# Moving the maximum and the low part's subtraction of the first MLP's weight conversions from VectorE to GpSimd

## The chip, the cores and the metric

One core of one Trainium2 chip runs the whole program. The metric is device time in microseconds of that core, the median over several runs. The engines are named as in the profile: PE (matmuls), PEld (its weight loads), DVE (VectorE), ACT (ScalarE), POOL (GpSimd) and SP (SyncE, which issues most of the DMAs).

## What is computed

An attention with 32 global and 512 local tokens for each of 4 batches and 8 heads of 64, with a window of 32 for the local queries, and then two MLPs over the 2176 rows of the result. Cut to what matters:

```python
s_g = scale * q_g @ k_all.T;  out_g = softmax(s_g) @ v_all
s_l = [scale * q_l @ k_g.T, where(|i-j| <= 32, scale * q_l @ k_l.T, -1e9)]
out_l = softmax(s_l) @ [v_g, v_l]
x = concat([out_g, out_l]) as rows of 8*64 = 512
h = x @ w_in          # 512 -> 2048, first MLP
x = max(0.01*h, h) @ w_out
h = x @ w2_in         # second MLP
x = (h - tanh(h)) @ w2_out
```

The weights of both MLPs come as 64-bit floats: each element is a low and a high 32-bit word.

## The kernel before

**Split numbers.** Every large matmul is made of three: an operand is held as a high part (rounded to the type that PE reads at full rate) and a low part (what the rounding left), and high times high, low times high and high times low are summed in PSUM. `split_w` makes the two parts of a weight: a copy on ACT (L138) and a subtraction (L139).

**Conversion.** A weight block of 128 rows by 512 arrives as pairs of words. `convert_w` turns it into 32-bit floats in five steps, each over 128x512: the absolute value of the high word on ACT (L123, into `wf`), the maximum with a tiny number (L124), a shift and mask (L125, into `wt`), the sign from the high word (L129) and the top bits of the low word (L132, back into `wf`); the last four are on DVE. `wf` has two buffers and `wt` one. `in_job` converts and splits a block of the first MLP's input weights into a `win` tile that stays; `out_job` does the same for the output weights, into `woh` (four buffers) and `wol` (three), which are also stored to DRAM by two SP DMAs (L711, L712) for later use. There are 16 blocks of each kind, so 32 such conversions. The second MLP's 32 blocks go through the same `convert_w`, called from `w2_job`, and are split later by `w2_place`.

**Attention.** It goes in 32 steps (`stage(s)`, counted from 0): a step is a pair of heads in one half of a sequence. For each, PE transposes keys and queries (`kps`, `qps`) and makes the scores (`sps`); DVE takes their minimum (L386; from step 10 on L392 does this with the mask); ACT makes the exponentials in four pieces (L399); DVE adds a small number to the sums and takes the reciprocals (L408, L409); the normalization of `e` is on POOL for steps 0 to 7 (two instructions of L413) and on DVE from step 8 (four of L418); PE transposes the result (`ptps`, L429), which is copied to `pt` by DVE or ACT (L432, L434); PE multiplies with the values (`avps`), and ACT and DVE split the outcome into `xh` and `xl` (L459, L461). Global queries run beside it (`sgps`, `gtps`, `gavps`; L528 to L532 on DVE, L529 on ACT, L567 and L568 for their split). `e` has two buffers that the steps take in turn.

**Order of the work.** The first ten steps run alone, with one `in_job` in each from step 2 on. Then the first MLP starts, with the rest of the attention woven between its matmuls: an item is one block of 128 hidden rows for a chunk of up to 512 tokens (`h`, then g on ACT and DVE by L201 to L203, and two items later `y`). During the first chunk each item also brings one `in_job`, for a block eight items ahead, and one `out_job`, for the block whose `y` comes about an item later. The second MLP's conversions follow in later items. PE's order is fixed by the order of the code up to the second MLP; on DVE, ACT, POOL and SP a scheduler places the instructions by its own costs, and each engine then runs its own list strictly in order. `converted` places a conversion after the last `avps` split and the last exponential issued so far.

Of the kernel before, what the change touches and what calls it, by code (L numbers as in the profile page):

```python
# [14 lines left out]
TINY = 2.0**-15  # L15
# [6 lines left out]
def kernel(  # L22
# [14 lines left out]
    nc = tc.nc  # L37
# [31 lines left out]
    def win_tile(f):  # L69
        t = persist.tile([128, 2, DM], F32R, tag=f"win{f}", name=f"win{f}")  # L70
        win_h[f], win_l[f] = [t[:, k].rearrange("p (k n) -> p k n", k=ND) for k in range(2)]
        return t
# [21 lines left out]
    def f32(t):  # L94
        return t.bitcast(F32)
# [18 lines left out]

    nw = [0]

    def convert_w(raw):
        hw, lw = raw[:, :, 1], raw[:, :, 0]
        t = mlp.tile([128, DM], I32, tag="wt", name="wt", bufs=1)
        w = mlp.tile([128, DM], F32, tag="wf", name="wf", bufs=2)  # L120
        nw[0] += 1

        nc.scalar.activation(w, hw.bitcast(F32), AF.Abs)  # L123
        nc.vector.tensor_scalar_max(w, w, TINY)  # L124
        nc.vector.tensor_scalar(  # L125
            out=t, in0=w.bitcast(I32), scalar1=3, scalar2=0x3FFFFFFF,
            op0=ALU.logical_shift_left, op1=ALU.bitwise_and,
        )
        nc.vector.scalar_tensor_tensor(  # L129
            out=t, in0=hw, scalar=-0x40000000, in1=t, op0=ALU.bitwise_and, op1=ALU.bitwise_or  # L130
        )
        nc.vector.scalar_tensor_tensor(  # L132
            out=w.bitcast(I32), in0=lw, scalar=29, in1=t, op0=ALU.logical_shift_right, op1=ALU.bitwise_or
        )
        return w

    def split_w(w, hi, lo, lo_engine):
        nc.scalar.activation(hi, w, AF.Copy)  # L138
        lo_engine.tensor_sub(lo, w, f32(hi))  # L139
# [6 lines left out]
    def wo_split(f, w):  # L146
        hi = mlp.tile([128, DM], F32R, tag="woh", name="woh", bufs=4)
        lo = mlp.tile([128, DM], F32R, tag="wol", name="wol", bufs=3)
        split_w(w, hi, lo, nc.vector)
        wo_t[f] = hi, lo  # L150

    def wo_fetch(f):
# [538 lines left out]
    def converted(raw):  # L691


        with tc.issue_after(last_av[0].ins), tc.issue_after(last_exp[0].ins):
            return convert_w(raw)

    def in_job():
        if in_raw:
            f, raw = in_raw.pop(0)
            w = converted(raw)  # L700
            t = win_tile(f)
            split_w(w, t[:, 0], t[:, 1], nc.vector)

    def out_job():
        if out_raw:
            f, raw = out_raw.pop(0)
            wo_split(f, converted(raw))
            hi, lo = wo_t[f]

            def store():  # L710
                nc.sync.dma_start(out=wo_dram[f][:, 0], in_=f32(hi))  # L711
                nc.sync.dma_start(out=wo_dram[f][:, 1], in_=f32(lo))  # L712

            later.append(store)
            out_load()
# [7 lines left out]
    def w2_job():  # L723
        if w2_raw:
            kind, f, raw = w2_raw.pop(0)
            with tc.issue_after(anchor[0].ins):
                w = convert_w(raw)
            dst = (w2i_dram if kind == "in" else w2o_dram)[f]
            later.append(lambda: nc.sync.dma_start(out=dst, in_=w))
        if w2_jobs:  # L730
            kind, f = w2_jobs.pop()
            w2_raw.append((kind, f, load_w(kind, w2_in if kind == "in" else w2_out, f)))
# [93 lines left out]
    if True:  # L826
# [16 lines left out]
        for pp in range(PRE):  # L843
            for op in stage(pp):
                op()
            in_load()
            if pp == 0:
                load_kq(2)
            if pp == 1:
                load_v(1)  # L850
            if pp >= 2:
                in_job()
            if pp == PRE - 2:
                out_load()
                out_load()
# [28 lines left out]
        for n in range(len(items) + 8):  # L884
            ph, c, f = items[n] if n < len(items) else (3, 0, 0)
            one = items[n - 1] if 0 < n <= len(items) else (3, 0, 0)
            if ph == 1:
                if c == 0:
                    in_load()
                    in_job()  # L890
                    if f > 0:
                        out_job()
                elif c == 4 and f == 0:
                    while gtodo:
                        gtodo.pop(0)()
                    att_ctx.close()
                    p2 = ctx.enter_context(tc.tile_pool(name="p2", bufs=1))
                    for k in range(NF - 1):
                        wo2_t.append([p2.tile([128, ND, 128], F32R, name=f"wo2{x}{k}") for x in "hl"])
                    wo2_t.append([x[1][:, :, 512:] for x in (xh, xl)])  # L900
                    x2_load(0, 0)
                    x2_load(0, 1)
                if c == 4 and 2 <= f < 2 + ND:
                    x2_split(0, f - 2)
            elif ph == 2 and order2.index(c) + 1 < 5:
                nx = order2[order2.index(c) + 1]
                if f in (2, 3):
                    x2_load(nx, f - 2)
                if 5 <= f < 5 + ND:
                    x2_split(nx, f - 5)  # L910
# [73 lines left out]
```

## Time and profile before

| | us |
|---|---|
| median of 3 runs | 955.41 |
| lowest and highest of the runs | 955.14, 955.56 |
| profiled execution: span from first to last instruction | 953.1 |
| PE busy in the span | 924.0 |
| DVE busy | 649.1 |
| ACT busy | 536.9 |
| POOL busy | 36.4 |

For the profiled execution the profile gives its span alone; the runs' median is 2.3 us above it. A busy time is an average over stretches with different limits, so the stretches are looked at one by one: the table of windows gives the busy time of each engine in each of them, the list of waits tells what ended an engine's idle time, and the timeline shows single instructions in order. The rows of these views that are used stand in a section of their own below.

### The profile page before, as it was taken

The page shows a single profiled execution, that of the slowest core. Times are in us where ns is not written, and L with a number is a line of the kernel's source. Part 1 is how long each engine was busy: PE and PEld are TensorE (multiplying, and loading weights), DVE is VectorE, ACT ScalarE, POOL GpSimd, SP SyncE. Part 2 cuts the span into 40 slices and gives each one's busy share as a digit, 9 for nine tenths or more (in the row PEclk, how much of TensorE's full clock was granted, in tenths as well). Part 3 has the DMA queues.
Part 4 walks back from the last instruction along what each step waited for, and adds up shares of the span by engine and source line. Part 5 has one row for each costly group of instructions (what it writes and reads, how often), then busy time and mean ns, then how long its engine had stood idle before and what let it go on. Part 6 is the DMA issues. An engine that isn't in the chain of part 4 may idle for free.

```text
span 953.1 us, 15441 instructions
## 1 busy us (share of the span) xinstructions
PE 924.0 (97%) x5436; PEld 769.9 (81%) x5436; DVE 649.1 (68%) x1429; ACT 536.9 (56%) x1223; POOL 36.4 (4%) x67
## 2 busy tenths in 40 slices
PE   7788999999999999999999999999999999999998
PEld 4565778787778777778999999888888888899997
DVE  3988996643366666664212348978888888888886
ACT  5676776655454554455323457556555655656565
POOL 5210000000000000000000000000000000000022
PEclk9898999999999999999999999999999999999999
DMA  8895556584368778676665674001100100010010
GB/s 203 231 268 148 174 162 187 172 235 148 105 204 254 251 215 264 209 252 189 212 198 189 208 237 160 2 1 34 45 1 0 67 1 1 1 45 1 1 34 23
DMA packets 144942, 127.12 MB, mean 133 GB/s; under 512 B 89184, under 2 KB 107616, under 8 KB 144864
## 3 DMA queue, kind: packets, MB, share of 16 engines
q1 hardware_dynamic: 142208, 125.47, 43.5%
q10 hardware_dynamic: 2656, 0.66, 0.3%
q8 instruction: 43, 0.70, 0.3%
q14 instruction: 35, 0.29, 0.1%
HBM read 100.40 MB, written 25.69 MB: 132 GB/s over the span
## 4 chain that ended last, share of the span: by engine, by line
PE 86%; DMA 6%; DVE 3%; ACT 3%; SPq 1%; issue 1%; POOL 0%; ACTq 0%; DVEq 0%
PE h L55 37%; PE o L55 20%; PE y L55 18%; PE sps L55 3%; PE avps L55 2%; PE ptps L429 2%; PE sgps L55 1%; DMA w2id<-wf 1%; DMA wraw<-in_moe_w_in_dram 1%; ACT e L399 1%; DMA w2od<-wf 1%; PE gavps L55 1%; PE kps L330 1%; ACT wf L123 1%; DMA vn<-in_v_l_dram 1%
## 5 line engine op out<-in xcount | busy, mean ns | idle before, releaser
L55 PE MATMUL h<-xh,win 128*128 128x512 f32 (+2 forms) x1280 | 357.8, 363 | 2.3 <-ACT g L201 2.3
L55 PEld LDWEIGHTS h<-xh,win 128*128 128x128 f32 x1280 | 228.6, 189 | 36.0 <-ACT g L201 3.2
L55 PE MATMUL h<-xl,win 128*128 128x512 f32 (+2 forms) x640 | 230.2, 360 | 0.0
L55 PEld LDWEIGHTS h<-xl,win 128*128 128x128 f32 x640 | 121.0, 189 | 16.1
L55 PE MATMUL y<-gh,woh 128*128 128x512 f32 (+2 forms) x320 | 121.3, 379 | 0.0
L203 DVE TENSOR_TENSOR gl<-g,gh 128x512 fp32r<-128x512 f32 (+2 forms) x80 | 48.7, 609 | 102.5 <-ACT gh L202 102.3
L55 PE MATMUL y<-gh,wol 128*128 128x512 f32 (+2 forms) x320 | 114.6, 358 | 0.0
L55 PE MATMUL y<-gl,woh 128*128 128x512 f32 (+2 forms) x320 | 114.0, 359 | 0.0
L55 PE MATMUL o<-wo2l,gh 128*128 128x512 f32 x255 | 99.6, 391 | 0.0
L55 PE MATMUL o<-wo2h,gh 128*128 128x512 f32 x255 | 99.4, 390 | 0.0
L55 PE MATMUL o<-wo2h,gl 128*128 128x512 f32 x255 | 97.7, 390 | 0.0
L609 ACT ACTIVATE u<-h 128x512 f32<-128x512 f32 (+2 forms) x80 | 42.6, 533 | 93.3 <-PE h L55 86.4
L201 ACT ACTIVATE g<-h 128x512 f32<-128x512 f32 (+2 forms) x80 | 42.2, 528 | 55.8 <-PE h L55 55.3
L55 PEld LDWEIGHTS y<-gh,woh 128*128 128x128 f32 x320 | 60.3, 188 | 12.6 <-issue 6.5
L634 ACT ACTIVATE gh<-p 128x512 fp32r<-128x512 f32 (+2 forms) x80 | 45.4, 568 | 41.1 <-DVE p L618 41.1
L123 ACT ACTIVATE wf<-wraw 128x512 f32<-128x512 f32 x48 | 31.6, 666 | 64.3 <-DMA w2od<-wf 15.6
L55 PEld LDWEIGHTS y<-gl,woh 128*128 128x128 f32 x320 | 60.2, 188 | 8.4
L55 PEld LDWEIGHTS y<-gh,wol 128*128 128x128 f32 x320 | 60.5, 189 | 5.6
L635 DVE TENSOR_TENSOR gl<-p,gh 128x512 fp32r<-128x512 f32 (+1 forms) x64 | 41.9, 654 | 21.7 <-ACT gh L634 21.7
L615 ACT ACTIVATE u<-u,consts 128x512 f32<-128x512 f32 (+2 forms) x80 | 52.7, 659 | 6.8 <-DVE p L613 4.1
L55 PEld LDWEIGHTS o<-wo2h,gl 128*128 128x128 f32 x255 | 47.9, 188 | 10.2
L55 PEld LDWEIGHTS o<-wo2h,gh 128*128 128x128 f32 x255 | 47.9, 188 | 9.0
(108 smaller groups left out, 1459.1 us busy)
## 6 DMA issues: line engine op xcount, KB each, us to landing
wraw<-in_moe_w_out_dram SPq DMA_DIRECT2D x32, 512.0 KB, 4.4
woh<-wod SPq DMA_DIRECT2D x64, 256.0 KB, 3.7
wol<-wod SPq DMA_DIRECT2D x64, 256.0 KB, 3.3
inraw<-in_moe_w_in_dram SPq DMA_DIRECT2D x16, 512.0 KB, 5.6
wraw<-in_moe_w_in_dram SPq DMA_DIRECT2D x16, 512.0 KB, 4.6
vr<-in_v_l_dram SPq DMA_DIRECT2D x48, 96.0 KB, 3.0
kr<-in_k_l_dram SPq DMA_DIRECT2D x47, 96.0 KB, 3.0
vn<-in_v_l_dram SPq DMA_DIRECT2D x32, 128.0 KB, 3.8
```

The source lines that it names most:

```text
L55: nc.tensor.matmul(o, lhsT, rhs, start=start, stop=stop)
L123: nc.scalar.activation(w, hw.bitcast(F32), AF.Abs)
L201: nc.scalar.activation(g[:, :N], h[:, :N], AF.Prelu, alpha=0.01)
L203: anchor[0] = nc.vector.tensor_sub(gl[:, :N], g[:, :N], f32(gh)[:, :N])
L330: nc.tensor.transpose(ps[:, c : c + n], kr[:n, t].rearrange("p h d -> p (h d)"), ident[:n, :n])
L399: last_exp[0] = nc.scalar.activation(e[:, h, j, s0 : s0 + n], x, AF.Exp, bias=st[:, k : k + 1], scale=-1.0, accum_out=st[:, 4 + k : 5 + k],)
L429: nc.tensor.transpose(ps[:, k * 128 : (k + 1) * 128], e[:, h, j, c0 : c0 + 128], ident)
L609: nc.scalar.activation(u, h, AF.Square)
L615: nc.scalar.activation(u, u, AF.Square, bias=tc_a2)
L634: nc.scalar.activation(gh[:, :N], p, AF.Copy)
L635: eng["pool" if i == order2[-1] else "dve"].tensor_sub(gl[:, :N], p, f32(gh)[:, :N])
```

## The change

`convert_w` takes the engine of its maximum as an argument, which is DVE unless something else is given. `converted`, the way by which both jobs of the first MLP come to it, gives POOL; `w2_job` calls `convert_w` without it and stays on DVE. The low part's subtraction of both jobs goes to POOL too. Nothing else of the conversion moves.

```diff
-    def convert_w(raw):
+    def convert_w(raw, max_engine=nc.vector):
...
         nc.scalar.activation(w, hw.bitcast(F32), AF.Abs)
-        nc.vector.tensor_scalar_max(w, w, TINY)
+        max_engine.tensor_scalar_max(w, w, TINY)
...
     def wo_split(f, w):
...
-        split_w(w, hi, lo, nc.vector)
+        split_w(w, hi, lo, nc.gpsimd)
...
         with tc.issue_after(last_av[0].ins), tc.issue_after(last_exp[0].ins):
-            return convert_w(raw)
+            return convert_w(raw, nc.gpsimd)
...
     def in_job():
...
-            split_w(w, t[:, 0], t[:, 1], nc.vector)
+            split_w(w, t[:, 0], t[:, 1], nc.gpsimd)
```

The scheduler then places the instructions of DVE, ACT, POOL and SP anew; PE's list is the same. Three places of it are used below. Names: `st` are small tiles of one step's minima and sums, `inraw` the raw blocks of input weights, `sps` scores, `avps` and `gavps` outcomes of attention, `gst` and `sg` the global softmax.

On DVE, before the change, from the small steps of attention step 3 over the conversion and the reductions of step 4:

```order
L408 TENSOR_SCALAR st<-st 128x4
L409 RECIPROCAL st<-st 128x4
L124 TENSOR_SCALAR wf<-wf 128x512
L125 TENSOR_SCALAR wt<-wf 128x512
L129 SCALAR_TENSOR_TENSOR wt<-inraw_280,wt 128x512
L386 TENSOR_REDUCE st<-sps 128x2 x2
L132 SCALAR_TENSOR_TENSOR wf<-inraw_280,wt 128x512
L461 TENSOR_TENSOR xl_69<-avps,xh_67 128x256
```

The same stretch on DVE with the change, from the reductions of step 3 to those of step 4:

```order
L386 TENSOR_REDUCE st<-sps 128x2 x2
L125 TENSOR_SCALAR wt<-wf 128x512
L129 SCALAR_TENSOR_TENSOR wt<-inraw_215,wt 128x512
L408 TENSOR_SCALAR st<-st 128x4
L132 SCALAR_TENSOR_TENSOR wf<-inraw_215,wt 128x512
L409 RECIPROCAL st<-st 128x4
L432 COPY pt<-ptps 128x512
L461 TENSOR_TENSOR xl_69<-avps,xh_67 128x256
L125 TENSOR_SCALAR wt<-wf 128x512
L129 SCALAR_TENSOR_TENSOR wt<-inraw_280,wt 128x512
L386 TENSOR_REDUCE st<-sps 128x2 x2
```

The reductions of step 3 (the first row with the change) now stand directly behind the split of `avps`, ahead of their step's conversion; those of step 4 still stand behind L125 and L129 of a conversion, now with no L124 and no L139 in the list.

On POOL, before, the normalizations of steps 2 to 5 (`e` buffers in turn) and the two memsets of `e`; numbers are the buffers' own:

```order
L413 TENSOR_TENSOR e0_132<-e0_132,st_376 128x512 x2
L381 MEMSET e0_132 128x2x32
L413 TENSOR_TENSOR e1_133<-e1_133,st_449 128x512 x2
L381 MEMSET e1_133 128x2x32
L413 TENSOR_TENSOR e0_132<-e0_132,st_537 128x512 x2
```

The same on POOL with the change:

```order
L413 TENSOR_TENSOR e0_132<-e0_132,st_376 128x512 x2
L124 TENSOR_SCALAR wf_421<-wf_421 128x512
L381 MEMSET e0_132 128x2x32
L124 TENSOR_SCALAR wf_499<-wf_499 128x512
L413 TENSOR_TENSOR e1_133<-e1_133,st_449 128x512 x2
L139 TENSOR_TENSOR win0_427<-wf_421,win0_427 128x512
L381 MEMSET e1_133 128x2x32
L413 TENSOR_TENSOR e0_132<-e0_132,st_537 128x512 x2
L139 TENSOR_TENSOR win1_505<-wf_499,win1_505 128x512
L124 TENSOR_SCALAR wf_580<-wf_580 128x512
L124 TENSOR_SCALAR wf_669<-wf_669 128x512
L413 TENSOR_TENSOR e1_133<-e1_133,st_609 128x512 x2
```

Maxima and subtractions now stand between the normalizations: the one of step 3 (`st_449`) behind the maximum of the second conversion, that of step 5 (`st_609`) behind two maxima and a subtraction.

On DVE, before, from L408 of step 7 to the last small step ahead of the reductions of step 8:

```order
L408 TENSOR_SCALAR st<-st 128x4
L409 RECIPROCAL st<-st 128x4
L528 TENSOR_REDUCE gst<-sg 128x1
L432 COPY pt<-ptps 128x512
L124 TENSOR_SCALAR wf<-wf 128x512
L568 TENSOR_TENSOR xl_70<-gavps,xh_68 128x32 x2
L125 TENSOR_SCALAR wt<-wf 128x512
L530 TENSOR_SCALAR gst<-gst 128x1
L129 SCALAR_TENSOR_TENSOR wt<-inraw_577,wt 128x512
L531 RECIPROCAL gst<-gst 128x1
L132 SCALAR_TENSOR_TENSOR wf<-inraw_577,wt 128x512
L532 TENSOR_SCALAR sg<-sg,gst 128x544
```

With the change, the same steps on DVE, from L408 of step 7 to the reductions of step 8:

```order
L408 TENSOR_SCALAR st<-st 128x4
L129 SCALAR_TENSOR_TENSOR wt<-inraw_496,wt 128x512
L409 RECIPROCAL st<-st 128x4
L528 TENSOR_REDUCE gst<-sg 128x1
L568 TENSOR_TENSOR xl_70<-gavps,xh_68 128x32
L432 COPY pt<-ptps 128x512
L132 SCALAR_TENSOR_TENSOR wf<-inraw_496,wt 128x512
L568 TENSOR_TENSOR xl_70<-gavps,xh_68 128x32
L530 TENSOR_SCALAR gst<-gst 128x1
L531 RECIPROCAL gst<-gst 128x1
L532 TENSOR_SCALAR sg<-sg,gst 128x544
L386 TENSOR_REDUCE st<-sps 128x2 x2
```

With the change an earlier conversion (`inraw_496`, not `inraw_577`) is in work here; it begins ahead of L408, and its last step L132 stands between two copies, ahead of the global softmax and of the reductions of step 8.

## Rows read from the trace of the kernel before

**Rows 1.** The page's first line: the span.

```profile
span 953.1 us, 15441 instructions
```

**Rows 2.** Windows: length, busy time (and instructions) of each engine, granted clock, DMA.

```profile
20.96:71.28 50.32, 40.46 (x366) 30.24 (x364) 46.39 (x91) 35.13 (x116) 13.68 (x14) 0.90 0.89 250
71.28:92.00 20.72, 16.27 (x119) 11.87 (x118) 19.82 (x53) 16.11 (x39) 0.00 (x0) 0.86 0.69 170
92.00:240.00 148.00, 148.00 (x945) 115.68 (x944) 97.51 (x282) 92.82 (x231) 0.46 (x3) 1.00 0.59 176
240.00:953.00 713.00, 704.12 (x3909) 601.68 (x3907) 480.62 (x992) 381.47 (x801) 12.39 (x19) 1.00 0.36 114
```

**Rows 3.** Waits of PE, stages 3 to 9: total us, times, longest.

```profile
PE sps L55 <- ACT e L399: 3.3, 3, 1.7
PE qps L339 <- ACT e L399: 2.5, 2, 1.5
```

**Rows 4.** Waits of PE, 71.28 to 92 us.

```profile
PE h L55 <- ACT g L201: 1.1, 1, 1.1
PE gavps L55 <- DVE xl L568: 0.7, 1, 0.7
```

**Rows 5.** Timeline, stage 4: start us, us, engine, line, operation.

```profile
28.29 0.20 ACT L399 ACTIVATION_READ_ACCUMULATOR e<-sps,st 128x1 f32 x1
...
29.05 2.22 POOL L413 TENSOR_TENSOR e<-e,st 128x512 f32<-128x512 f32 x2 [2.48 <-ACT wf L123]
...
29.07 1.29 DVE L124 TENSOR_SCALAR wf<-wf 128x512 f32<-128x512 f32 x1 [0.17 <-ACT wf L123]
...
30.40 1.15 DVE L125 TENSOR_SCALAR wt<-wf 128x512 int32<-128x512 int32 x1
...
31.58 0.69 DVE L129 SCALAR_TENSOR_TENSOR wt<-inraw,wt 128x512 int32<-128x512 int32 x1
...
32.19 1.15 DVE L386 TENSOR_REDUCE st<-sps 128x2 f32<-128x448 f32 x2
...
32.90 0.45 ACT L399 ACTIVATE e<-sps,st 128x224 f32<-128x224 f32 x1 [1.33 <-DVE st L386]
...
34.75 0.20 ACT L399 ACTIVATION_READ_ACCUMULATOR e<-sps,st 128x1 f32 x1
```

**Rows 6.** Line L124: min/median/max ns; then timeline near the end, DVE beside POOL.

```profile
L124 DVE TENSOR_SCALAR wf<-wf x64: 416/422/1296, 22.2 to 434.4; 128x512 f32<-128x512 f32 x64
...
913.60 0.74 POOL L635 TENSOR_TENSOR gl<-p,gh 128x256 fp32r<-128x256 f32 x1 [2.07 <-ACT gh L634]
...
913.99 0.63 DVE L616 SCALAR_TENSOR_TENSOR p<-s,p 128x256 f32<-128x256 f32 x1
```

**Rows 7.** Groups on DVE, stages 3 to 9: count | busy us, mean ns.

```profile
L139 DVE TENSOR_TENSOR win<-wf,win 128x512 fp32r<-128x512 f32 x6 | 5.8, 964 | 0.1
...
L124 DVE TENSOR_SCALAR wf<-wf 128x512 f32<-128x512 f32 x7 | 5.7, 821 | 0.4 <-ACT wf L123 0.3
```

**Rows 8.** Groups on POOL, whole span.

```profile
L413 POOL TENSOR_TENSOR e<-e,st 128x512 f32<-128x512 f32 x16 | 17.5, 1111 | 32.1 <-ACT wf L123 10.4 <-ACT kt L332 7.5 <-DVE st L409 5.3
...
L635 POOL TENSOR_TENSOR gl<-p,gh 128x256 fp32r<-128x256 f32 x16 | 11.8, 738 | 553.9 <-ACT gh L634 552.0 <-issue 1.9
...
L260 POOL TENSOR_SCALAR_AFFINE_SELECT mask<-mask 128x96 bf16<-128x96 bf16 x6 | 1.5, 265 | 0.0
...
L260 POOL TENSOR_SCALAR_AFFINE_SELECT mask<-mask 128x192 bf16<-128x192 bf16 x2 | 0.7, 345 | 0.0
```

**Rows 9.** Timeline: one low part of an output weight, and its matmul.

```profile
115.33 0.69 DVE L139 TENSOR_TENSOR wol<-wf,woh 128x512 fp32r<-128x512 f32 x1
...
118.34 0.39 PE L55 MATMUL y<-gh,wol 128*128 128x512 f32 x1
```

**Rows 10.** Windows: 4 us before the clock fell, and 4 us of it.

```profile
84.00:88.00 4.00, 2.50 (x26) 1.63 (x22) 3.90 (x9) 2.69 (x7) 0.00 (x0) 0.78 0.70 155
88.00:92.00 4.00, 3.77 (x9) 2.81 (x9) 3.93 (x8) 3.07 (x7) 0.00 (x0) 0.50 0.76 251
```

## Prediction

> **What bounds the kernel now.** Read the span first [rows 1]: 953.1 us of the profiled execution. The runs have a median of 955.41 us, 2.3 us more, which I take for what lies around the span; every sum below is made on the span and carried over to 955.41. A measurement of this kernel can tell about 0.2%, 1.9 us, from no change.
>
> Then cut the span into stretches and look at each engine in each [rows 2]. A "stage" is one attention step (a pair of heads in half a sequence); I count its length from the end of its predecessor's fourth exponential on ACT to the end of its own. The first row holds stages 3 to 9: 50.32 us for seven, 7.19 us each. There PE works 40.46 us, ACT 35.13, DVE 46.39, POOL 13.68. The second row is the start of the first MLP: DVE 19.82 of 20.72 us. From 92 us on PE is busy in every microsecond to 240 us (148.00 of 148.00), and it is the bound to the end but for 9 us (704.12 of 713). So only the first 92 us can get shorter; behind them, a change can only cost.
>
> What PE waits for in those stretches is what an edit has to shorten. In stages 3 to 9 [rows 3] it stands for exponentials on ACT (3.3 and 2.5 us); in the start of the MLP [rows 4] for ACT, and 0.7 us for a DVE subtraction. To see why the exponentials are late, follow stage 4 in time [rows 5]. It begins at 28.49 us, where the last exponential of stage 3 ends (28.29 + 0.20). DVE then runs L124, L125 and L129 of a weight conversion, and only behind them, at 32.19, the two reductions L386 that the exponentials wait for; the last exponential ends at 34.95. **DVE's queue, with a conversion ahead of the reductions, is what sets this stage's 6.46 us.** And those conversion steps are slow there: L124 takes 1.29 us and L125 1.15 us, while POOL runs its two normalizations L413, 2.22 us from 29.05. L124 takes 0.42 us in the median over the kernel [rows 6]. Far later the same is seen with two inputs: L616 starts at 913.99, while POOL's L635 runs until 914.34, and takes 0.63 us. So a DVE instruction of this kind waits until POOL's instruction is through.
>
> **What the change moves.** 32 conversions (16 of each weight matrix of the first MLP) send L124 and L139 to POOL: 64 instructions. In stages 3 to 9 that takes seven L124 and six L139 off DVE, by the group rows 5.7 + 5.8 = 11.5 us [rows 7], and leaves DVE 46.4 - 11.5 = 34.9 us of work in 50.3. In the second stretch the same kind of step goes, on a DVE that is nearly always busy.
>
> On POOL the two are new. The subtraction: POOL's L635 has two inputs too and takes 738 ns for 256 columns, L413 takes 1111 ns for 512 with one input spread from a small tile [rows 8]. For 512 columns of two full inputs the ends are 1.11 and 2 x 0.738 = 1.48 us; I take 1.25, between them, since the selects next to it show that POOL's steps have a fixed start. The maximum has one input: the selects grow from 265 to 345 ns between 96 and 192 columns, 0.83 ns a column, which makes 345 + 320 x 0.83 = 611 ns at 512; the upper end is L413's 1.11. I take 0.62. POOL then has 13.68 + 7 x 0.62 + 6 x 1.25 = 25.5 us in the 50.3: not full.
>
> A rule speaks against the change. The rows show POOL's two-input step at nearly double DVE's time (1.25 us by the estimate above; 0.69 us for L129, a DVE step of the same size and two inputs) [rows 5, 8]. The Trainium skill (GPSIMD Engine Reference, Engine selection) says that elementwise work belongs on VectorE, GpSimd being about twice as slow with two inputs. By that rule alone each conversion gets later by some 0.8 us and the kernel slower; the sum here goes by who waits, and the later result is waited for by nobody on the short path, as follows.
>
> **Stage by stage.** The order shown above puts the reductions of stage 3 straight behind the step before, and it does so in stage 5 too. Then DVE no longer decides, and I take ACT's own 35.13 / 7 = 5.0 us plus 0.5 for hand-overs: 5.5 us each. Stage 4 gets worse: L125 and L129 still stand ahead of its reductions, and L125 now waits for POOL. ACT's first conversion step ends about 1.0 us in (0.6 as now [rows 5], and one copy of 0.4 that the new order puts ahead of it); the maximum on POOL ends at 1.65, the two L413 behind it run to 3.9, L125 gets through between them, L129 behind them to 4.6, the first reduction to 5.2 and the exponentials (32.90 to 34.95 now, 2.05 us [rows 5]) to 7.2. Stage 6 has its maximum done early and waits for ACT, which has a 1 us pass of the global heads more: 6.4. Stage 7 has the copies of the global heads on ACT and PE: 7.2. Stage 8 has the third step of a conversion (L132), POOL's two L413 and the next maximum in a row ahead of its reductions: 2.2 + 0.6 + 0.7 us behind a start at 1.1, then 0.8 of small steps, 0.6 for the first reduction and 2.05 for the exponentials, which is 8.05; 8.2 with hand-overs. Stage 9 stays at 5.6. **Sum: 5.5 + 7.2 + 5.5 + 6.4 + 7.2 + 8.2 + 5.6 = 45.6 us, against 50.3: 4.7 us gained.** A hand-made chain leaves hand-overs out, 0.1 us for each of seven stages: 4.0. In the second stretch I count only the 0.7 us that DVE's own subtraction holds PE up [rows 4]; the 1.1 us for ACT's L201 may go or stay. That makes 4.7 us: **950.7 us**. With both POOL prices at their upper ends, 2.59 us a conversion for 1.87, the seven stages lose up to 5.0 us again, and nothing is left (955.7); with the lower ends, 1.72, a further microsecond is gained.
>
> **Behind 92 us** I count nothing. What covers the later results: a low part `wol` is ready at 116.0 us and its matmul runs at 118.3 [rows 9], 2.3 us of slack, of which the new path takes 0.2 + 0.6 us and two hand-overs. POOL has nothing else there (0.46 us in 148 [rows 2]). If the slack were less, every one of the 16 row blocks would be late by what is missing. ACT's next first step waits for a free `wf` (two buffers), so for POOL's subtraction instead of DVE's; g and its copies queue behind it on ACT, with two row blocks of lead. On SP the store of `wol` now waits for POOL, and weight loads and keys queue behind it, by the same 1 us. POOL issues no DMA of its own, and its last memsets of `e` are not urgent.
>
> **Rivals.** (a) *The stages are held elsewhere.* ACT's and PE's chain or the shared stretch with POOL takes up what DVE gives; for it: PE's own work is 40.46 of 50.32 us, at a clock of 0.90 of full speed; against it: the reductions of stage 4 visibly wait for DVE alone. Time: 954 to 957. (b) *POOL stands in the way, and it gets slower.* The mechanism is the one of [rows 5]: what shares the way to the data waits for POOL's whole instruction. If in stages 4, 6 and 8 the steps ahead of the reductions meet one maximum and one subtraction more than I counted, that is 3 x 1.87 = 5.6 us, and stages 3 to 9 come to 51.2, 0.9 us worse than now; in the second stretch six subtractions end 0.56 us later each (1.25 - 0.69) with ACT behind them, of which I count 2 us. Time: 958.3. It decides as soon as POOL is found busy when L125 or L132 arrives in most stages. The Trainium skill (SBUF — State Buffer, Who interferes with whom) states this as a rule: such an instruction blocks for the whole of the other. The trace agrees, by the 1.29 and 1.15 us above. (c) *More is gained.* PE's clock fell to half speed (0.50) from 88 to 92 us [rows 10], after PE had been busy for only 2.50 of the 4 us before; its nine matmuls there fill 3.77 us, about half of which is the clock's. If a fuller PE keeps the clock and the stages come to 5.8 us each, PE's 40.46 / 7, the gain is 9.9 + 2 us: 943.5. (d) That the change does not do what it says: the order shows all 64 instructions on POOL, so no.
>
> **How the numbers follow.** The forecast, 2 to 9 us faster, 0.62; (c) 0.06; (a) 0.18; (b) 0.14. Hence faster by over 0.2%: 0.68; within: 0.18; slower: 0.14. The time is that of the forecast. The range leaves out half of (c) and most of (b): 945.5 to 956.5 holds the forecast, (a) but for its edge, and both ends of POOL's prices.
>
> **What would show it.** Right: stages 3 to 9 end near 67 us instead of 71.28, with stage 3 and stage 5 near 5.5 us and stage 4 no shorter than now; DVE some 35 us busy in them; L139 on POOL near 1.25 us and L124 near 0.62; PE busy without a gap from some 87 us to 235. Wrong: L413 starting more than 1.5 us after its reciprocal in most stages, reductions L386 that still follow a blocked L125 or L129, or PE waiting behind 92 us for `wol`, `win` or g.

## The result and the profile after

The changed kernel takes **961.82 us** (median of 4 runs, 961.49 to 962.2); the kernel before took 955.27 us beside it (4 runs, 954.36 to 955.56). The ratio is 1.0076, 95% interval 1.0058 to 1.0094: slower by some 6.5 us, where 4.7 us less were forecast. The profiled execution has a span of 959.7 us for 953.1 [rows 1].

The windows of the profile after, in the columns of [rows 2], and then of [rows 10], four microseconds longer:

```profile
20.96:71.28 50.32, 40.66 (x366) 29.72 (x364) 39.93 (x83) 37.45 (x120) 33.40 (x28) 0.90 0.88 250
71.28:92.00 20.72, 16.76 (x112) 11.85 (x113) 17.28 (x33) 13.16 (x33) 14.27 (x11) 0.76 0.58 142
92.00:240.00 148.00, 145.05 (x906) 112.20 (x904) 99.48 (x236) 89.96 (x223) 58.74 (x44) 0.99 0.59 175
240.00:953.00 713.00, 709.34 (x3940) 605.66 (x3940) 481.54 (x1000) 384.89 (x808) 11.71 (x18) 1.00 0.35 114
...
84.00:88.00 4.00, 2.91 (x26) 1.87 (x26) 3.56 (x6) 2.01 (x4) 2.79 (x3) 0.66 0.15 34
88.00:92.00 4.00, 3.06 (x8) 2.17 (x9) 2.74 (x5) 3.31 (x8) 3.19 (x3) 0.50 0.58 185
92.00:96.00 4.00, 4.00 (x15) 2.57 (x14) 2.33 (x6) 0.67 (x2) 2.61 (x2) 0.56 0.47 147
```

DVE was relieved only in part: 39.93 us in the first row, where 34.9 were forecast, because its other steps got longer and five more of them fall into the row (83 instructions for 91 less 13). POOL has 33.40 us instead of the forecast 25.5. From 92 to 240 us, where before PE was busy in every microsecond, it now stands for 2.95 us.

What POOL's two new steps cost, in the columns of [rows 8]:

```profile
L124 POOL TENSOR_SCALAR wf<-wf 128x512 f32<-128x512 f32 x32 | 50.3, 1576 | 52.0 <-ACT wf L123 48.1 <-DMA inraw<-in_moe_w_in_dram 2.3 <-DMA vr<-in_v_l_dram 0.8
L139 POOL TENSOR_TENSOR win<-wf,win 128x512 fp32r<-128x512 f32 x16 | 22.6, 1411 | 6.1 <-ACT win L138 3.9 <-PE qps L339 2.1
L139 POOL TENSOR_TENSOR wol<-wf,woh 128x512 fp32r<-128x512 f32 x16 | 20.8, 1299 | 25.4 <-ACT woh L138 16.2 <-PE y L55 9.1
```

The maximum, taken as 0.62 us, has a mean of 1.58 us. The subtraction, taken as 1.25, is near it: 1.30 to 1.41.

**Where the time went.** PE has the same instructions in the same order in all the kernels told of here (but for two swaps of neighbouring weight loads near 45 us in e8_order and e12_order_wf3), so its weight loads can be paired one to one. The table is worked out from the profiled executions: how much later (negative: earlier) the same weight load of PE starts than in the kernel before, at a given time of the kernel before. One execution stands for each kernel. It differs from the median of its kernel by 2 us at most, for e11_chain by 3.4 (967.63 us for 971.02), so a difference of a microsecond or two shows nothing by itself.

```
us in the kernel before     46     55     66     76     95    118    140    240    600    940
after                     -5.8   -0.3   -4.8   -1.0    1.9    1.9    6.3    6.3    6.5    6.5
e1_sub_only                0.1   -0.0    0.3    0.2    3.6    3.6    5.0    5.0    4.0    4.0
e2_max_only               -3.1    1.5   -3.0   -1.1    0.1    0.0    1.9    2.1    2.0    2.0
e3_stages                 -5.7   -0.1   -4.5   -1.1    0.3    0.2    0.2    0.2    2.7    2.7
e4_mlp                    -0.2   -0.6    0.4    0.4    0.8    1.4    4.4    6.2    5.2    5.2
e5_wf3                    -2.5    1.9   -2.4    1.6    2.1    7.8   10.0   10.0   10.8   10.8
e6_before_wf3             -0.0   -0.0   -0.0    0.5   -3.5   -3.5   -3.5   -2.8   -2.7   -2.7
e8_order                  -5.7   -1.5   -5.8   -5.9   -4.7   -4.7   -4.7   -4.7   -5.6   -5.6
e10_dummy                 -1.6    3.5   -1.0   -0.3    2.7    7.7   13.4   15.6   15.3   15.3
e11_chain                 -0.8    2.6   -1.6   -1.0   -2.1    3.8   12.6   13.7   12.7   12.7
e12_order_wf3             -6.6   -2.2   -6.6   -6.2  -10.0  -10.0  -10.0  -10.0   -9.2   -9.2
e13_copy                  -6.1   -3.2   -7.6   -4.1   -1.8   -0.7    1.0    2.0    2.9    2.9
```

The first line tells the story. PE is ahead by 5.8 us at 46 and 4.8 us at 66 us. That is lost twice: 6.7 us between 66 and 95 us, in the last stage and at the start of the MLP, and another 4.4 between 118 and 140 us. In the stages the lead dips as well, at 55 us, and comes back. By the prediction's own measure, the end of the fourth exponential of stage 9, the stages end at 69.26 us for 71.28: 2.0 us are gained in them, where 4.0 to 4.7 were forecast.

PE's waits in the profile after (columns as in [rows 3]), from 71.28 to 92 us and from 92 to 165:

```profile
PE gavps L55 <- DVE xl L568: 2.1, 1, 2.1
PE qps L339 <- ACT pg L544: 1.5, 1, 1.5
PE qps L339 <- ACT pt L434: 1.2, 1, 1.2
PE h L55 <- ACT g L201: 0.6, 1, 0.6
...
PE ptps L429 <- DVE xl L461: 2.0, 1, 2.0
PE h L55 <- ACT g L201: 0.4, 1, 0.4
PE sgps L55 <- DVE st L392: 0.4, 1, 0.4
```

PE waits neither for `wol` nor for `win`, but for attention steps of ACT and DVE that have conversions in front of them. The timeline shows how (start, length, engine, line; in brackets the wait), in five places: stage 6, stage 9 (from 63.07 us), the start of the MLP, and two places behind it (from 127.06 and from 134.00 us).

```profile
39.75 1.99 POOL L124 TENSOR_SCALAR wf<-wf 128x512 f32<-128x512 f32 x1 [0.69 <-ACT wf L123]
...
41.71 2.43 POOL L413 TENSOR_TENSOR e<-e,st 128x512 f32<-128x512 f32 x2
...
43.01 0.66 PE L429 MATMUL ptps<-ident,e 128*128 128x128 f32 x4 [2.00 <-POOL e L413]
...
44.10 1.71 POOL L139 TENSOR_TENSOR win<-wf,win 128x512 fp32r<-128x512 f32 x1
...
44.61 1.50 DVE L532 TENSOR_SCALAR sg<-sg,gst 128x544 f32<-128x544 f32 x1
...
46.25 0.66 PE L541 MATMUL gtps<-ident,sg 128*128 128x128 f32 x2 [1.03 <-DVE st L408]
...
63.07 1.49 POOL L124 TENSOR_SCALAR wf<-wf 128x512 f32<-128x512 f32 x1 [2.31 <-DMA inraw<-in_moe_w_in_dram]
...
63.95 2.44 DVE L418 TENSOR_SCALAR e<-e,st 128x192 f32<-128x192 f32 x4
...
64.52 1.26 POOL L139 TENSOR_TENSOR win<-wf,win 128x512 fp32r<-128x512 f32 x1
...
66.31 1.14 DVE L386 TENSOR_REDUCE st<-sps 128x2 f32<-128x448 f32 x2
...
81.58 1.27 POOL L139 TENSOR_TENSOR win<-wf,win 128x512 fp32r<-128x512 f32 x1
...
82.88 0.67 ACT L123 ACTIVATE wf<-wraw 128x512 f32<-128x512 f32 x1 [2.24 <-POOL win L139]
...
84.20 0.66 PE L55 MATMUL gavps<-pg,vn 128*64 128x32 f32 x16 [2.09 <-DVE xl L568]
...
85.80 1.27 POOL L139 TENSOR_TENSOR win<-wf,win 128x512 fp32r<-128x512 f32 x1 [0.41 <-ACT win L138]
85.89 1.74 DVE L129 SCALAR_TENSOR_TENSOR wt<-wraw,wt 128x512 int32<-128x512 int32 x1
...
87.11 0.68 ACT L123 ACTIVATE wf<-inraw 128x512 f32<-128x512 f32 x1 [0.90 <-POOL win L139]
...
127.06 1.29 POOL L139 TENSOR_TENSOR wol<-wf,woh 128x512 fp32r<-128x512 f32 x1
...
127.12 1.51 DVE L125 TENSOR_SCALAR wt<-wf 128x512 int32<-128x512 int32 x1 [1.38 <-POOL wf L124]
...
128.39 0.67 ACT L123 ACTIVATE wf<-wraw 128x512 f32<-128x512 f32 x1 [1.95 <-POOL wol L139]
...
134.00 1.49 POOL L124 TENSOR_SCALAR wf<-wf 128x512 f32<-128x512 f32 x1 [1.59 <-ACT wf L123]
...
134.26 2.58 DVE L418 TENSOR_SCALAR e<-e,st 128x224 f32<-128x224 f32 x4
...
135.46 1.26 POOL L139 TENSOR_TENSOR wol<-wf,woh 128x512 fp32r<-128x512 f32 x1
...
137.82 0.66 PE L429 MATMUL ptps<-ident,e 128*128 128x128 f32 x4 [2.01 <-DVE xl L461]
```

The same four L418 of stage 9 in the kernel before:

```profile
67.19 1.04 DVE L418 TENSOR_SCALAR e<-e,st 128x192 f32<-128x192 f32 x4
```

Three things are to be seen. POOL's maximum runs ahead of the normalization L413 on POOL's own queue, and PE waits 2.00 us for it (39.75 to 43.01). A DVE step that starts while a POOL step runs stands until that one is through: L125, 0.42 us by itself, takes 1.51 (127.12), and L129 takes 1.74 for 0.69 (85.89). The normalization on DVE, L418, meets the maximum and the subtraction in turn and takes 2.44 and 2.58 us for 1.04; in stage 9 the reductions L386 stand behind it, and at 134 us it is what makes `xl` late, for which PE has its longest wait behind 92 us (2.01, at 137.82). And ACT's next first step L123 stands 2.24, 0.90 and 1.95 us until POOL's subtraction has freed `wf`, with all that is queued behind it on ACT. Behind the idle stretches PE's clock is at its lower level, 0.50 of full speed from 88 to 92 us and 0.56 from 92 to 96; in the kernel before it was 0.50 [rows 10] and then 0.87 there.

### The profile page after: what moved, and what is told of

Its sections match the earlier page's. It is cut to its first block, busy times and chain, and to the rows that moved or that the text cites. A ratio compares the mean times of both kernels' runs of the same rounds, so it can differ in the third digit from the quotient of the medians.

```text
span 959.7 us, 15468 instructions
## 1 busy us (share of the span) xinstructions
PE 929.3 (97%) x5436; PEld 771.7 (80%) x5436; DVE 644.1 (67%) x1365; ACT 538.2 (56%) x1223; POOL 128.8 (13%) x131
## 2 busy tenths in 40 slices
DMA packets 144942, 127.12 MB, mean 132 GB/s; under 512 B 89184, under 2 KB 107616, under 8 KB 144864
## 3 DMA queue, kind: packets, MB, share of 16 engines
q1 hardware_dynamic: 142208, 125.47, 42.5%
## 4 chain that ended last, share of the span: by engine, by line
PE 77%; DMA 8%; DVE 6%; ACT 3%; POOL 2%; issue 2%; SPq 2%; ACTq 0%; POOLq 0%; DVEq 0%
PE h L55 34%; PE o L55 19%; PE y L55 15%; PE sps L55 2%; DMA wraw<-in_moe_w_out_dram 2%; DMA wraw<-in_moe_w_in_dram 2%; PE avps L55 2%; PE ptps L429 2%; DMA w2od<-wf 1%; POOL wf L124 1%; DVE wt L129 1%; DVE wf L132 1%; DVE wt L125 1%; DMA w2id<-wf 1%; ACT e L399 1%
## 5 line engine op out<-in xcount | busy, mean ns | idle before, releaser
L203 DVE TENSOR_TENSOR gl<-g,gh 128x512 fp32r<-128x512 f32 (+2 forms) x80 | 52.0, 650 | 104.7 <-ACT gh L202 104.7
L635 POOL TENSOR_TENSOR gl<-p,gh 128x256 fp32r<-128x256 f32 x16 | 11.8, 741 | 555.5 <-ACT gh L634 553.6
L123 ACT ACTIVATE wf<-wraw 128x512 f32<-128x512 f32 x48 | 31.7, 669 | 67.0 <-DMA w2od<-wf 15.9
L124 POOL TENSOR_SCALAR wf<-wf 128x512 f32<-128x512 f32 x32 | 50.3, 1576 | 52.0 <-ACT wf L123 48.1
```

The source lines that it names most:

```text
L124: max_engine.tensor_scalar_max(w, w, TINY)
L203: anchor[0] = nc.vector.tensor_sub(gl[:, :N], g[:, :N], f32(gh)[:, :N])
L635: eng["pool" if i == order2[-1] else "dve"].tensor_sub(gl[:, :N], p, f32(gh)[:, :N])
```

## The experiments

**Which of the two instructions.** One half of the change each: in the first only the subtraction is on POOL, in the second only the maximum.

```diff
-            return convert_w(raw, nc.gpsimd)
+            return convert_w(raw)
```

> Only the subtraction of the 32 conversions is on POOL; the maximum is back on DVE. Theory M (the maximum is the costly part: 1.49 us on POOL where it meets nobody, against 0.42 on DVE, and it stands ahead of the normalizations and in the middle of every conversion): the loss of the change is gone, 951 to 956 us. Theory P (any two-input work on POOL holds DVE's two-input steps up, so the 1.26 us subtraction costs as much as the maximum): half of the loss or more stays, 958 to 961 us.

Measured: 960.16 us against 953.96 of the kernel before, ratio 1.0079 (1.0057 to 1.0102). The ratios are given as recorded, with their 95% intervals; they are not exactly the quotients of the two medians. Theory M falls with this run, theory P holds in it.

```diff
-        split_w(w, hi, lo, nc.gpsimd)
+        split_w(w, hi, lo, nc.vector)
...
-            split_w(w, t[:, 0], t[:, 1], nc.gpsimd)
+            split_w(w, t[:, 0], t[:, 1], nc.vector)
```

> Only the maximum is on POOL; the subtraction is back on DVE. Theory M: most of the loss stays, 958 to 963 us, with the maximum at 1.5 us or more. Theory P: each conversion loses one of two POOL steps, so about half, 957 to 959 us.

Measured: 958.37 us, 1.0067 (1.0041 to 1.0092), which fits either theory. By the ratios each half alone costs about what both cost (in the table, of one execution each, the maximum alone costs less), and the dear maximum is not the sole culprit. The table adds something: with the subtraction alone nothing is gained in the stages (0.1 us at 46 us), with the maximum alone 3.1. Only the second has reductions L386 of the stages ahead of the conversion on DVE, in stages 3, 5, 8 and 9.

**Which stretch.** POOL only for the 8 conversions of the attention-only stages, and then only for the 24 behind them, with a switch that both jobs read (its two values are swapped in the second run).

```diff
+    low_engine = [nc.gpsimd]
...
-            return convert_w(raw, nc.gpsimd)
+            return convert_w(raw, low_engine[0])
...
         tags[0] = run_tags
+        low_engine[0] = nc.vector
```

> Both steps on POOL for the eight conversions issued in the attention-only steps; all later ones as before on DVE. Two theories on the place. Place S (the first 70 us are not slower with the change, its loss is made in the first MLP chunk, where two conversions an item run through POOL): 952 to 956 us, no worse than before. Place B (the loss is made in both stretches): 957 to 959 us.

Measured: 957.24 us, 1.004 (1.0021 to 1.0058): the time of place B.

> The complement: the eight conversions of the attention-only steps on DVE as before, the other 24 on POOL. Place S: the whole loss and the gain of the steps missing, 960 to 965 us, and PE idle behind 92 us. Place B: 957 to 959 us.

Measured: 960.6 us, 1.0084 (1.0062 to 1.0106): the time of place S, so neither theory on the place fits both runs. By the table, the 24 conversions behind the stages lose 5.4 us between 95 and 240 us. The 8 in the stages gain 4.5 us up to 66 us and have lost them by 95; that run is level until 240 us and falls 2.5 us back between 240 and 600 us, in code that the edit does not touch, for which I have no cause (other kernels shift by up to 1.0 us there, either way). So the two losses of the change have two owners. The one from 66 to 95 us, 6.7 us, comes mostly with the 8 conversions of the stages: it is 4.8 us in e3_stages, where POOL has only the last steps of these left to do, and 0.4 in e4_mlp. The one behind 95 us comes with the 24: it is 5.4 us in e4_mlp and nothing in e3_stages up to 240 us.

**What holds the result up.** If ACT's wait for `wf` were the loss, a third buffer would end it. Every third conversion of the first MLP gets one of its own; the same edit to the kernel before is the control.

```diff
-        w = mlp.tile([128, DM], F32, tag="wf", name="wf", bufs=2)
+        if nw[0] % 3 == 2 and nw[0] < 2 * NF:
+            w = att.tile([128, DM], F32, tag="wfa", name="wfa", bufs=1)
+        else:
+            w = mlp.tile([128, DM], F32, tag="wf", name="wf", bufs=2)
```

> The change with a third buffer for the converted row block (every third conversion of the first MLP's weights writes a buffer of its own, which the attention's memory has room for). Theory W (ACT's next first step L123 waits for GpSimd's subtraction to free `wf`, and what queues behind it on ACT arrives late): the loss behind 66 us shrinks to a third, PE is at most 2.5 us behind the kernel before at 240 us, 955 to 957.5 us. Theory C (the conversion's chain itself is longer, and its VectorE steps stand until GpSimd's instruction is through): the third buffer changes little, PE is 4.5 us or more behind at 240 us, 959 to 962 us.

> The kernel before with the same third buffer, as the control of the run above. Both theories: 953 to 957 us, PE within 1.5 us of the kernel before at 240 us.

Measured: 965.03 us, 1.0107 (1.0074 to 1.014), and for the control 953.28 us, 0.9991 (0.9971 to 1.0011). Theory W falls: with a third buffer the change gets no better, 10.0 us behind at 240 us; the time lies above theory C's range too, but the two kernels' intervals overlap, so that it got worse is not shown. The control's time is as expected; its profiled execution is 2.8 us ahead at 240 us, where at most 1.5 were expected, and has no half clock from 84 to 92 us, but the runs show no gain. The wait for `wf` stands in the timeline, but it was not what cost the time; PE's greatest waits from 71 to 165 us are now for DVE's attention steps, `xl` 3.6 us and `st` 2.7. I take it that conversions freed of the wait start earlier and stand in front of these; that is not shown.

**Is it the order or the engine that helps in the stages?** The kernel before, both steps on DVE, with one addition: a stage's conversion is issued behind the next stage's two reductions (`last_red`), as the change had come to order them in some of the stages (not in stage 4). Here every one of stages 3 to 9 has it so; ACT's steps of the conversion move with it.

```diff
-        nc.vector.tensor_scalar_max(w, w, TINY)
+        with tc.issue_after(last_red[0].ins) if held[0] else nullcontext():
+            nc.vector.tensor_scalar_max(w, w, TINY)
...
-            for op in stage(pp):
+            for n, op in enumerate(stage(pp)):
+                exp = last_exp[0]
                 op()
+                if n == 1 and pp >= 3:
+                    exp, last_exp[0] = last_exp[0], exp
+                    held[0] = True
+                    in_job()
+                    held[0] = False
+                    last_exp[0] = exp
...
-            if pp >= 2:
+            if pp == PRE - 1:
                 in_job()
```

> The kernel before (maximum and subtraction on VectorE), with the conversions of the attention stages issued behind the next stage's two reductions L386, so that the reductions stand ahead of the conversion in VectorE's queue, as the change had them. Theory O (the 4.8 to 5.8 us that the change was ahead at 46 and 66 us come from the order alone): PE is 3 to 6 us ahead of the kernel before at 46 and 66 us, and of it at least 2 us are left at 240 us: 949 to 953 us. Rival R (the relief of VectorE by GpSimd gave them): under 1.5 us ahead at 46 us, 954 to 958 us.

Measured: **949.56 us**, 0.995 (0.9929 to 0.9971), 5.7 and 5.8 us ahead at 46 and 66 us and 4.7 at 240. Theory O holds in every number. Its windows have no POOL work but the normalization, and PE is again gapless from 92 us on:

```profile
20.96:71.28 50.32, 42.70 (x387) 31.28 (x384) 44.03 (x103) 39.06 (x126) 12.91 (x14) 0.93 0.87 248
71.28:92.00 20.72, 17.11 (x120) 12.94 (x120) 19.14 (x52) 13.79 (x36) 0.00 (x0) 0.84 0.71 176
92.00:240.00 148.00, 148.00 (x948) 116.34 (x948) 95.33 (x272) 92.48 (x228) 0.61 (x4) 1.00 0.59 178
```

DVE has 44.03 us of work in the stages, hardly less than before [rows 2], and PE is as far ahead as with the change. What gained the time was that the reductions went first, not that DVE was relieved: e1_sub_only, with the relief of the subtraction in the old order, gains nothing there. What is left of PE's waiting from 71 to 100 us is 3.3 us for a transfer (`vg`) and 0.2 for g.

**What single steps cost on POOL.** Extra instructions on two spare tiles beside the third chunk of the first MLP.

```diff
+                        g.tensor_scalar_max(pa, pa, TINY)
+                        g.tensor_scalar_max(pb, pa, TINY)
+                        g.tensor_scalar_max(pa[:, :256], pa[:, :256], TINY)
+                        g.tensor_scalar_add(pa, pa, 1.0)
...
+                        g.tensor_tensor(out=pa, in0=pa, in1=pb, op=ALU.add)
+                        g.tensor_sub(pa, pa, pb)
+                        g.tensor_sub(pa[:, :256], pa[:, :256], pb[:, :256])
+                        g.tensor_copy(pb, pa)
```

> The kernel before with extra instructions on GpSimd alone, on two spare tiles, beside the first MLP's third chunk: maximum with a constant (in place, into another tile, 256 columns), addition of a constant, addition and subtraction of two tiles (512 and 256 columns), a copy. Theory P (the maximum's price of 1.49 us is that of any one-input operation with a constant on GpSimd): addition of a constant takes 1.4 to 1.6 us too, in place or not, and the two-input ones 1.25 us. Rival Q (the price is that of the maximum, or of writing in place): addition of a constant, or the maximum into another tile, takes under 1.2 us. The time of the whole is not read.

Its groups, with the least, the median and the greatest ns of one, in the order of the diff (without the subtraction of 512 columns, 1.28 us at the least):

```profile
L961 POOL TENSOR_SCALAR probea<-probea x8: 1490/1537/1926, 7.3 to 126.5; 128x512 f32<-128x512 f32 x8
...
L962 POOL TENSOR_SCALAR probeb<-probea x8: 1484/1708/2044, 8.9 to 128.1; 128x512 f32<-128x512 f32 x8
...
L963 POOL TENSOR_SCALAR probea<-probea x8: 843/917/2042, 10.4 to 131.6; 128x256 f32<-128x256 f32 x8
...
L964 POOL TENSOR_SCALAR probea<-probea x8: 1493/1582/1971, 11.4 to 133.7; 128x512 f32<-128x512 f32 x8
...
L966 POOL TENSOR_TENSOR probea<-probea,probeb x8: 1264/1334/1710, 12.9 to 135.5; 128x512 f32<-128x512 f32 x8
...
L968 POOL TENSOR_TENSOR probea<-probea,probeb x8: 727/980/1178, 17.9 to 138.6; 128x256 f32<-128x256 f32 x8
...
L969 POOL COPY probeb<-probea x8: 610/718/1016, 18.7 to 139.8; 128x512 f32<-128x512 f32 x8
```

Theory P holds: a step with a constant takes 1.49 us at the least, in place or not, maximum or addition; two tiles take 1.26; a copy takes 0.61, just what I had worked out for the maximum from the selects. From 256 to 512 columns the maximum grows by 0.65 us, which is 2.5 ns a column, three times the selects' 0.83 [rows 8].

**Held up, or only later?** Two runs on the kernel before part these for the 24 conversions behind the stages. In the first POOL works beside the conversion and nobody waits for it (but ACT once, 0.6 us, for a `woh` that POOL still reads), with the lists of DVE and ACT the same as before; in the second it lengthens the chain with one-column steps that hardly touch data, and the scheduler moves the lists of DVE and ACT with it.

```diff
         lo_engine.tensor_sub(lo, w, f32(hi))
+        if extra:
+            nc.gpsimd.tensor_sub(extra[0], extra[0], f32(hi))
+            nc.gpsimd.tensor_scalar_max(extra[0], extra[0], TINY)
```

> The kernel before, in which GpSimd does a subtraction and a maximum more for each of the 24 conversions behind the attention-only stages: on a spare tile, reading the finished high part, with nobody waiting for their result. Every other engine has the same instructions in the same order as before. Theory S (GpSimd's instructions hold VectorE's up, and that alone costs the time): PE is 4 us or more behind the kernel before at 160 us, 957 to 961 us. Theory C (the conversion's own chain is longer, load beside it costs little): under 1.5 us behind at 160 us, 952 to 955.5 us.

```diff
+        for _ in range(tiny[0]):
+            nc.gpsimd.tensor_scalar_max(w[:, :1], w[:, :1], TINY)
         nc.vector.tensor_scalar_max(w, w, TINY)
...
+        for _ in range(tiny[0] // 2):
+            nc.gpsimd.tensor_sub(lo[:, :1], w[:, :1], f32(hi)[:, :1])
         lo_engine.tensor_sub(lo, w, f32(hi))
```

> The kernel before, in which the same 24 conversions pass through GpSimd only for a delay: six maxima of one column ahead of VectorE's maximum and three subtractions of one column ahead of VectorE's subtraction, so the chain of each conversion is longer by some 1 to 2 us while GpSimd touches almost no data; VectorE keeps all its work, and the order on the engines moves as it does with a longer chain. Theory C: PE is 3 us or more behind the kernel before at 160 us, 956.5 to 961 us. Theory S: under 1.5 us behind, 952 to 955.5 us.

Measured: 970.39 us, 1.0157 (1.0134 to 1.018), and 971.02 us, 1.017 (1.0145 to 1.0194), against 954.99. Both lose far more than either theory had. Groups of DVE from 92 to 140 us (count | busy us, mean ns | idle ahead of them), of the kernel before, then of the first, then of the second run (where L139 is L144 and L129 is L132):

```profile
L139 DVE TENSOR_TENSOR wol<-wf,woh 128x512 fp32r<-128x512 f32 x5 | 3.4, 684 | 0.0
```

```profile
L139 DVE TENSOR_TENSOR wol<-wf,woh 128x512 fp32r<-128x512 f32 x5 | 6.4, 1283 | 0.0
L129 DVE SCALAR_TENSOR_TENSOR wt<-inraw,wt 128x512 int32<-128x512 int32 x5 | 5.2, 1042 | 0.1
```

```profile
L144 DVE TENSOR_TENSOR wol<-wf,woh 128x512 fp32r<-128x512 f32 x5 | 3.4, 690 | 4.0 <-POOL wol L143 4.0
L132 DVE SCALAR_TENSOR_TENSOR wt<-inraw,wt 128x512 int32<-128x512 int32 x5 | 3.5, 692 | 0.1
```

Here the two ways are apart. With a bystander on POOL, DVE's subtraction takes 1.28 us for 0.68 with no idle time; with the longer chain it takes its 0.69 and DVE stands idle. Holding up alone is enough to stop PE, in unchanged lists; the longer chain is enough too, though with its moved lists. PE's greatest wait from 71 to 165 us is for `wol`, 5.4 us in the first and 8.3 in the second. DVE has no room there: it was busy 42.5 of the 48 us from 92 to 140 in the kernel before. The one-column steps were dearer than meant, 0.25 to 0.29 us each, some 2.3 us a conversion, so the two sizes can't be compared with each other. In the change PE never waits for `wol`; these two runs show what either way can do, not the share of each in the change. I take it that the change sits below both because it takes L124 and L139, 1.1 us, off DVE in return; no run shows that.

**Had the maximum cost what I took.** POOL's maximum replaced by a copy.

```diff
-        max_engine.tensor_scalar_max(w, w, TINY)
+        if max_engine is nc.gpsimd:
+            nc.gpsimd.tensor_copy(w, w)
+        else:
+            max_engine.tensor_scalar_max(w, w, TINY)
```

> The change with GpSimd's maximum of each conversion replaced by a copy of the same row block onto itself (0.61 us in the run of the single operations, against 1.49): what is left out is the clamp of the smallest weights. The order on VectorE moves a little with the shorter step. Theory M (the mis-sized maximum, 1.49 us for 0.62, is what cost the forecast): PE is 2 us or more ahead of the kernel before at 240 us, 948 to 953 us. Theory S (any step of that kind on GpSimd, of 0.6 and 1.3 us, lengthens the chain and holds VectorE up at the start of the MLP): PE is level or behind at 240 us, 954 to 960 us.

Measured: 956.2 us, 1.0024 (1.0003 to 1.0045), and 2.0 us behind at 240 us. Theory S holds: even at the forecast price (the copy's mean is 0.67 us) the gain does not last. The stages are better, 44.6 us for the change's 48.6, and PE is 7.6 us ahead at 66 us; then 5.8 us are lost by 95 us and 3.8 more by 240.

**Both edits that leave the work on DVE.**

> Both edits that left VectorE's work where it is: the conversions of the stages behind the next stage's reductions, and the third buffer for the converted row block. If PE's half clock at the start of the MLP is the next loss and the buffer removes it, as it did in the control run: 946 to 949.5 us; if the two gains are the same one: 949 to 952 us.

Measured: **946.4 us**, 0.9913 (0.9892 to 0.9934): the order of e8_order with the third buffer of e5_wf3, faster than both kernels.

```profile
20.96:71.28 50.32, 42.70 (x389) 31.49 (x388) 43.20 (x104) 39.09 (x125) 13.79 (x14) 0.93 0.90 252
71.28:92.00 20.72, 19.63 (x158) 15.00 (x158) 20.55 (x62) 17.26 (x45) 0.00 (x0) 1.00 0.77 183
```

From 71 to 92 us PE has 19.63 of 20.72 us at full clock, where the order alone had 17.11 at 0.84. So the buffer that did not help the change seems to help here (the intervals of the two ratios just touch); why it helps the one and not the other is not shown.

## Why the prediction was wrong

**What bounds the kernel: right.** Only the first 92 us could get shorter, and DVE's conversion ahead of the reductions is what set the stages; e8_order shows it with all the work left on DVE.

**The stages: right in part, for another reason.** My sum went by the order that came with the change, but I took that order and the 11.5 us that DVE is rid of for one gain. e8_order has the order without the relief, and its stages 3 to 9 take 45.6 us together. That this is just the sum forecast for the change is luck: its stage 7 takes 10.5 us, and others make up for it. With the change the stages came to 5.2, 7.8, 4.4, 5.2, 11.2, 7.2 and 7.6 us, together 48.6 where 45.6 were forecast. Stages 3, 5, 6 and 8 beat their numbers, stage 4 is worse by 0.6 (the maximum takes 0.9 more). Stage 7, forecast at 7.2, is the largest miss, and POOL is not its main cause, though POOL's queue held the normalization behind a maximum there and DVE's L532 stood behind POOL's subtraction: in e8_order, with no conversion step on POOL, it takes nearly as long. In both, PE runs at half clock in it, until 54 us with the change and 52 in e8_order. The clock by itself seems to move several microseconds there: e10_dummy and e11_chain, whose stages have the order of before, swing from 1.6 or 0.8 ahead to 3.5 or 2.6 behind, with the half clock from 48.5 to 58.7 us in e10_dummy where the kernel before has it from 41.9 to 48.7. Stage 9, which was to stay at 5.6, is worse by 2.0, and this is POOL's: L418 stood for its maximum and its subtraction (2.44 us for 1.04), with the reductions behind it, while e8_order has 4.9 us there.

**The maximum at 0.62 us: mis-sized, 1.49 unhindered.** The upper end of 1.11 was too low as well. The selects, another kind of operation and on bf16, were the wrong row to take the growth from: they grow by 0.83 ns a column, a step with a constant by 2.5. By e13_copy this term is worth some 4 us, nearly all of it in the stages: 6.3 less 2.0 at 240 us, and 48.6 less 44.6 in the stages (the order moves a little with it).

**"The later result is waited for by nobody", and "behind 92 us I count nothing": the steps that failed.** I had weighed the slack of `wol` [rows 9], and it did hold: PE never waits for `wol` or `win` in the profile after. But DVE was nearly full there (42.5 of 48 us from 92 to 140), with attention steps in the same queue, and each DVE step that stood for POOL, the attention's own L418 among them, made those late. From the end of the stages on I forecast a gain of 0.7 up to 92 us and nothing behind it. The change went from 2.0 us ahead there to 1.9 behind at 95 us, and lost 4.4 more behind that. Even with the maximum at the forecast price, e13_copy loses 9.6 us from 66 to 240 us. A slack of one result is not the slack of the queues that it passes through.

**Rival (b) had the mechanism, with a place and a size too small.** DVE's steps stand for POOL's whole instruction: 1.51 us for 0.42 and 1.74 for 0.69 here. I priced it at 0.9 us in the stages and 2 in the second stretch, at nothing behind 92 us, and gave it 0.14. That a step blocks for the whole of the other engine's instruction is what the Trainium skill (SBUF — State Buffer, Who interferes with whom) says, and the trace agrees. I had set aside, with the argument that failed, a second rule, that elementwise work belongs on VectorE, GpSimd being about twice as slow with two inputs (the Trainium skill, GPSIMD Engine Reference, Engine selection). The runs bear it out: the subtraction takes 1.26 us on POOL at the least and 0.69 on DVE. Of one input that section says roughly line rate, and there the runs decide otherwise: the maximum takes 1.49 us on POOL and 0.42 on DVE.

What stays open: why e3_stages falls back 2.5 us behind 240 us, why stage 7 gets so long with the reductions first, and how much of the change's own loss is holding up and how much is the longer chain; in the change they come together.

## What to carry to other kernels

Before work is moved to an idle engine, try the order alone: here the gain in the stages came with two short reductions that went ahead of a long conversion, and it needed no other engine. When a step in the middle of a chain moves to a slower engine, price it by a row of the same kind of operation, and count what it delays in every in-order queue that it passes through, not only the slack of its last result. An idle engine is no help to one that is nearly 90% busy if the two hold each other up.

## What I had not expected of the hardware

POOL needs longer for one tile and a constant (1.49 us for 128x512) than for two tiles (1.26), and both over twice as long as for a copy (0.61). A one-column step on POOL still takes 0.25 to 0.29 us.
